# An RWKV kernel with phase mixing on one core: planned dummy matmuls, r loaded two tokens to a partition, a planner that chooses engines and load order, and w spread by a one-row matmul

## The chip, the cores and the metric

The kernel runs on one core of a Trainium2 chip. The metric is the time of one execution on the device, in microseconds (us). Single executions of one kernel scatter by about 1% here, so kernels are compared by several runs. A few executions were slow (a lower granted clock, or a time more than 1.5% above the fastest run of the same kernel).

Engines are named as in the profile: PE is TensorE (PEld its weight loads), DVE is VectorE, ACT is ScalarE, POOL is GpSimd, SP is SyncE, which issues nearly all transfers.

## The reference, cut to what matters

```python
def _attn_ref(r, k, v, w, u):            # r, k, v: (4, 8, 768, 48)   w, u: (8, 48)
    for t in range(S):
        cur = einsum('bhd,bhe->bhde', u * k_t, v_t)
        y[:, :, t] = einsum('bhd,bhde->bhe', r_t, state + cur)
        state = w * state + einsum('bhd,bhe->bhde', k_t, v_t)

def _moe_ref(x, w_theta, w_tok_r, w_tok_i, w_ch):   # x: (4, 768, 384)
    theta = x @ w_theta
    zr, zi = x * cos(theta), x * sin(theta)
    y = einsum('ts,bsd->btd', w_tok_r, zr) + einsum('ts,bsd->btd', w_tok_i, zi)
    u = x + y
    return u + maximum(u @ w_ch, 0.0)
```

The recurrence is done in chunks of 128 tokens. r is scaled by powers of w and k by inverse powers. For each batch the "front" works on three pairs of chunks: load r, k, v; scale; transpose r and k on TensorE; scores; masks; state; output; then theta, sine and cosine. "Mixing" follows: 288 matmuls of 128x384 (the groups `zr,WrT` and `zi,WiT` in the profile), more transposes, the channel matmuls, and the store.

## The kernel before: the parts that the change touches

The instructions are not written in program order. Each task is added to a `Plan` with an engine, an assumed duration in ns, its dependences and the PSUM banks it takes. A list scheduler with these assumed durations puts the tasks in order, a random search changes their priorities and keeps what shortens the planned span, and the order that results is fixed for each engine. On the chip every engine then runs its own list strictly in order.

```python
LATENCY = {PE: 200.0, DVE: 150.0, ACT: 175.0, POOL: 160.0, SP: 2200.0}
ROUNDS = 2000
# ... (inside Plan.order: the best ready task of an engine; a bank-taking task needs free banks)
                        if t.ready <= now and (
                                not t.acq or len(t.acq) + t.keep <= nfree):
                            rank = (t.prio - (STAY if e == PE and t.mode == last_mode and last_mode else 0.0), t.seq)
# ... (Plan.search: the order of the loads is not searched)
        pool = [t for t in self.tasks if t.eng != SP]
# ... (tiles: w is loaded to all partitions, and its logarithm kept beside it)
    w_f = sb.tile([C, H, D], F32, name="w_f")
    lw_f = sb.tile([C, H, D], F32, name="lw_f")
# ...
    NL = 12
    Ls = ring(NL, [C, 2 * HD], F32, "ld")       # load buffers, 3072 bytes to a partition
# ... (setup)
        P.add(SP, 300, lambda: nc.sync.dma_start(out=w_f, in_=rows_of(w, C)),
              wr=["w_f"], prio=-2e6, lat=3000)
# ... (r, k and v: two transfers of 192 KB, runs of 48 floats = 192 bytes, 1050 ns assumed for each)
        for c in range(2):
            t0 = (2 * pr + c) * C
            P.add(SP, 1050, lambda c=c, t0=t0: nc.sync.dma_start(
                out=Ls[i][:, c * HD:(c + 1) * HD].rearrange("p (h d) -> p h d", h=H),
                in_=src[b, :, t0:t0 + C, :].transpose([1, 0, 2])),
                wr=[("L", i, c)], prio=pri, lat=2200)
# ... (weights: 500 ns for each 192 KB)
        P.add(SP, 500 * n, lambda: nc.sync.dma_start(
            out=Ls[i][:, :n * HD].rearrange("p (o c) -> p o c", o=n), in_=src),
            wr=L2(i), prio=pri, lat=2200)
# ... (transposes by TensorE, eight or six blocks of 128 columns to a bank; the copy out is always ACT's)
        P.add(PE, 56 * n, go, rd=rd + ["ident"], acq=[tok], prio=prio, mode=0)
        P.add(ACT, act_ns(n * C), lambda: nc.scalar.activation(
            dst, bank16(tok)[:, :n * C].rearrange("p (a c) -> p a c", a=n), Act.Copy),
            use=[tok], wr=wr, prio=prio)
# ... (front: the copy of v to bf16 is always ACT's, the scaling of k DVE's, that of r POOL's)
            P.add(ACT, act_ns(2 * HD, False), lambda vb=vb, iv=iv: nc.scalar.activation(
                vb.rearrange("p a h d -> p (a h d)"), Ls[iv], Act.Copy),
                rd=L2(iv), wr=[kv_], prio=pb + 1)
# ... (mixing: KEEP is 0, so a mix may take the last free bank)
                P.add(PE, 649, mix, ..., prio=pb, keep=KEEP)
# ... (the end)
    P.search(ROUNDS)
    ctx.enter_context(tc.manual_schedule())
    for t in P.order():
        t.fn()
```

## Time and profile before

The median of three runs was 149.66 us (148.32 to 149.67). The profiled run took 148.95 us, of which 147.2 lie between the first and the last instruction. TensorE is busy for 130.2 us of it, VectorE for 114.8, ScalarE for 92.0.

The page of the kernel before: first the busy time of each engine, then the span in 40 equal slices of 3.7 us, where each digit is the busy share in tenths, then the main DMA queue with its packets, MB and share of the 16 DMA engines' time.

```profile
span 147.2 us, 4185 instructions
...
PE 130.2 (89%) x1641; PEld 91.3 (62%) x1641; DVE 114.8 (78%) x220; ACT 92.0 (63%) x175; POOL 79.4 (54%) x96
...
PE   0157687999999999999989999999999999999990
...
DVE  0349869699954989999979999999899998442561
...
PEclk9999999999999999999999999999999999999999
DMA  2999988999999799899998997995000111120224
...
q1 hardware_dynamic: 81040, 24.98, 69.9%
```

TensorE is full from about the eighth slice on. Below full are the first 28 us. The DMA row is full in those same slices, and stays full for two thirds of the run.

The stretches 5 to 15, 15 to 28 and 28 to 42 us of the kernel before: length, busy us (and instructions) of each engine, granted clock, share of the DMA engines' time, GB/s.

```profile
core 0: us, PE busy (x) PEld busy (x) DVE busy (x) ACT busy (x) POOL busy (x), PEclk, DMA share, GB/s
5.00:15.00 10.00, 5.41 (x74) 4.14 (x75) 6.42 (x14) 6.32 (x11) 4.69 (x5) 1.00 1.12 221
15.00:28.00 13.00, 10.25 (x133) 8.42 (x130) 10.80 (x18) 9.54 (x17) 8.80 (x9) 1.00 0.94 261
28.00:42.00 14.00, 14.00 (x166) 11.73 (x166) 11.89 (x24) 11.69 (x27) 7.79 (x8) 1.00 0.99 309
```

(The share adds up the times of all packets that start in a stretch, so it can pass 1.)

The timeline of TensorE at the start of the kernel before: start, length, engine and line, operation, operands, and in brackets the idle time before it with what ended it.

```profile
7.20 1.04 PE L414 MATMUL bank_62<-ident,Rw_95 128*128 128x128 bf16 x8 [1.28 <-POOL Rw_95 L436]
8.65 1.07 PE L414 MATMUL bank_63<-ident,Kw_97 128*128 128x128 bf16 x8 [0.41 <-DVE Kw_97 L448]
11.41 0.29 PE L470 MATMUL bank_64<-RT_106,KT_110 64*128 64x128 bf16 x1 [1.69 <-ACT KT_110 L417]
```

Eight transposes take 1.04 us here and 0.61 us later in the run: TensorE starts at half rate. The PEclk row, at 9 throughout, does not show it.

The waits of TensorE from the first mix matmul (40.5 us) to its end, kernel before: waiter, what it waited for, us in total, times, longest.

```profile
PE bank_61 L581 <- ACT xT_142 L417: 0.7, 1, 0.7
PE bank_65 L489 <- DVE PD_113 L481: 0.2, 1, 0.2
```

Two waits in 103 us: from the first mix on, TensorE is the bound of this kernel.

### The profile page before, as it was taken

What the parts mean: (1) busy time and instruction counts of PE and PEld (TensorE: products, weight loads), DVE (VectorE), ACT (ScalarE), POOL (GpSimd) and SP (SyncE); (2) the same over time, 40 slices, a digit from 0 to 9 for tenths busy, and PEclk for the clock granted to TensorE, in tenths of its full rate; (3) what the DMA queues carried; (4) which work ended last, traced back from release to release, by engine and by line L of the source; (5) the groups of instructions that cost most, each with busy time, mean ns of one, the idle gap of its engine ahead of it and who ended that gap; (6) DMA issues with size and microseconds to landing.
All of it is one profiled execution on the core that took longest, in us unless ns stands there. A gap on an engine that the chain in (4) does not pass through costs nothing.

```text
span 147.2 us, 4185 instructions
## 1 busy us (share of the span) xinstructions
PE 130.2 (89%) x1641; PEld 91.3 (62%) x1641; DVE 114.8 (78%) x220; ACT 92.0 (63%) x175; POOL 79.4 (54%) x96
## 2 busy tenths in 40 slices
PE   0157687999999999999989999999999999999990
PEld 0036574879966776667746666677666666656640
DVE  0349869699954989999979999999899998442561
ACT  3484667878949368689473984899735467702140
POOL 7317937473735649868469779691552747400000
PEclk9999999999999999999999999999999999999999
DMA  2999988999999799899998997995000111120224
GB/s 71 225 216 223 255 188 299 296 393 403 224 178 196 172 192 222 182 220 237 181 235 160 203 219 176 229 224 184 4 0 0 58 53 58 53 107 0 73 92 160
DMA packets 81084, 25.24 MB, mean 172 GB/s; under 512 B 75561, under 2 KB 79529, under 8 KB 81065
## 3 DMA queue, kind: packets, MB, share of 16 engines
q1 hardware_dynamic: 81040, 24.98, 69.9%
q8 instruction: 13, 0.21, 0.6%
q14 instruction: 7, 0.05, 0.1%
q10 hardware_dynamic: 24, 0.00, 0.0%
HBM read 20.25 MB, written 4.72 MB: 170 GB/s over the span
## 4 chain that ended last, share of the span: by engine, by line
PE 74%; DVE 7%; ACT 7%; DMA 6%; issue 3%; SPq 1%; DVEq 0%; ACTq 0%
PE bank_64 L613 8%; PE bank_65 L613 7%; PE bank_68 L613 4%; DMA ld_87<-in_v_dram 3%; DMA ld_86<-in_r_dram 3%; PE bank_63 L613 3%; PE bank_62 L613 3%; PE bank_68 L414 2%; PE bank_63 L414 2%; PE bank_63 L581 2%; PE bank_67 L613 2%; PE bank_61 L629 2%; PE bank_66 L414 2%; PE bank_64 L581 1%; PE bank_66 L613 1%
## 5 line engine op out<-in xcount | busy, mean ns | idle before, releaser
L613 PEld LDWEIGHTS <-WrT 128*128 128x128 bf16 x144 | 14.0, 97 | 7.8
L613 PEld LDWEIGHTS <-WiT 128*128 128x128 bf16 x144 | 14.1, 98 | 7.2
L526 POOL TENSOR_TENSOR Z_122<-Y_120,wC 128x192 f32<-128x192 f32 x12 | 7.8, 649 | 7.2 <-DVE Y_120 L521 4.0
L613 PE MATMUL bank_64<-zr_135,WrT 128*128 128x384 bf16 x30 | 9.8, 326 | 0.0
L613 PE MATMUL bank_64<-zi_137,WiT 128*128 128x384 bf16 x30 | 9.8, 326 | 0.0
L526 POOL TENSOR_TENSOR Z_123<-Y_121,wC 128x192 f32<-128x192 f32 x8 | 4.9, 617 | 7.3 <-DVE Y_121 L523 7.3
L613 PE MATMUL bank_65<-zr_135,WrT 128*128 128x384 bf16 x24 | 7.8, 327 | 0.0
L613 PE MATMUL bank_65<-zi_137,WiT 128*128 128x384 bf16 x24 | 7.8, 326 | 0.0
L436 POOL TENSOR_TENSOR Rw_95<-ld_88,wpow 128x384 bf16<-128x384 f32 x4 | 4.8, 1208 | 4.2 <-PE bank_67 L414 4.2
L436 POOL TENSOR_TENSOR Rw_96<-ld_85,wpow 128x384 bf16<-128x384 f32 x6 | 5.9, 1004 | 0.7 <-DMA ld_85<-in_r_dram 0.7
L594 POOL TENSOR_TENSOR zi_137<-x_132,sin_139 128x384 bf16<-128x384 bf16 x4 | 3.7, 932 | 4.3 <-ACT sin_139 L585 4.3
L613 PE MATMUL bank_62<-zi_138,WiT 128*128 128x384 bf16 x18 | 5.9, 326 | 0.0
L613 PE MATMUL bank_62<-zr_136,WrT 128*128 128x384 bf16 x18 | 5.9, 326 | 0.0
L594 POOL TENSOR_TENSOR zi_137<-x_134,sin_139 128x384 bf16<-128x384 bf16 x4 | 3.8, 964 | 3.6 <-ACT sin_139 L585 3.6
L315 PE MATMUL bank_61<-ident_f,wu 8*128 8x8 f32 x1 | 0.2, 239 | 5.7 <-DMA wu<-in_u_dram 5.7
L581 PEld LDWEIGHTS <-xT_142 128*128 128x128 bf16 x36 | 3.3, 98 | 2.6 <-ACT xT_142 L417 0.8
L594 POOL TENSOR_TENSOR zi_138<-x_132,sin_140 128x384 bf16<-128x384 bf16 x4 | 3.6, 913 | 2.4 <-ACT sin_140 L585 2.3
L414 PEld LDWEIGHTS <-Rw_95 128*128 128x128 bf16 x48 | 3.6, 111 | 2.0 <-POOL Rw_95 L436 1.4
L581 PEld LDWEIGHTS <-xT_141 128*128 128x128 bf16 x36 | 3.5, 103 | 2.1 <-issue 0.3
L436 POOL TENSOR_TENSOR Rw_96<-ld_91,wpow 128x384 bf16<-128x384 f32 x4 | 4.0, 998 | 1.5 <-DMA ld_91<-in_r_dram 0.8
L470 PEld LDWEIGHTS <-KT_110 64*128 64x128 bf16 x96 | 3.1, 101 | 2.7 <-ACT KT_110 L417 2.0
L436 POOL TENSOR_TENSOR Rw_95<-ld_94,wpow 128x384 bf16<-128x384 f32 x4 | 4.3, 1071 | 0.8 <-DVE Kw_98 L448 0.8
(593 smaller groups left out, 505.1 us busy)
## 6 DMA issues: line engine op xcount, KB each, us to landing
out_dram<-fin_150 SPq DMA_DIRECT2D x8, 192.0 KB, 2.0
out_dram<-fin_149 SPq DMA_DIRECT2D x8, 192.0 KB, 3.1
out_dram<-fin_151 SPq DMA_DIRECT2D x8, 192.0 KB, 2.0
ld_85<-in_r_dram SPq DMA_DIRECT2D x6, 192.0 KB, 4.6
ld_86<-in_k_dram SPq DMA_DIRECT2D x6, 192.0 KB, 3.6
ld_87<-in_v_dram SPq DMA_DIRECT2D x6, 192.0 KB, 4.0
ld_88<-in_r_dram SPq DMA_DIRECT2D x4, 192.0 KB, 4.1
ld_89<-in_k_dram SPq DMA_DIRECT2D x4, 192.0 KB, 3.6
```

Of the source, the lines that this page charges most:

```text
L315: nc.tensor.matmul(bank("wu")[:, :2 * HP], wu.rearrange("p a d -> p (a d)"), ident_f[:2 * HP, :2 * HP], is_transpose=True, start=True, sto ...
L414: nc.tensor.matmul(bank16(tok)[:, i * C:(i + 1) * C], s, ident, is_transpose=True, start=(i == 0), stop=(i == n - 1))
L436: lambda c=c, vec=vec, Rw=Rw, ir=ir: vec.tensor_mul(Rw[:, c, :, :D], Ls[ir][:, c * HD:(c + 1) * HD].rearrange("p (h d) -> p h d", h=H), wpow),
L470: nc.tensor.matmul(bank(tk[hi])[:, hp * C:(hp + 1) * C], KT[q, c, hp, :], RT[q, c, hp, :], start=(hp == 0), stop=(hp == HP - 1))
L526: P.add(POOL, pool_ns(HP * D) - 70, lambda cc=cc: nc.gpsimd.tensor_mul(Zs[cc % 2], Ys[cc % 2], wide(wC, D)), rd=[("Y", cc % 2), "wC"], wr= ...
L581: nc.tensor.matmul(bank(th)[:, :HD], xT[:, t, dk, :], Wth[:, dk, :], start=(dk == 0), stop=(dk == ND - 1))
L594: P.add(POOL, pool_ns(HD), lambda sn=sn, to=to, t=t: nc.gpsimd.tensor_mul(zi[:, to], x[:, to], sn[:, t]), rd=xk + [("sin", g % 2, t)], wr= ...
L613: nc.tensor.matmul(bank(tm)[:, :HD], WT[:, so, to * C:(to + 1) * C], z[:, so], start=(so == 0 and i == 0), stop=(so == NCH - 1 and i == 1))
L629: nc.tensor.matmul(bank(tf)[:, :HD], uT[:, dk, :], Wch[:, dk, :], start=(dk == 0), stop=(dk == ND - 1))
```

## The change

Its intent: fill the gaps that the plan foresees on TensorE with dummy matmuls so that its clock rises early; halve the number of small packets of r; shorten the path to the powers of w; and let the search choose the engine of many copies and products, and the order and buffer of the loads. The parts of the diff that matter, with cuts marked (`...`):

```diff
-ROUNDS = 2000
-LATENCY = {PE: 200.0, DVE: 150.0, ACT: 175.0, POOL: 160.0, SP: 2200.0}
+LATENCY = {PE: 200.0, DVE: 130.0, ACT: 190.0, POOL: 130.0, SP: 2000.0}
+SLACK = 150.0
+FILL, MARGIN, COLD = 56.0, 200.0, 5000.0
+BEGIN = 800.0
+ROUNDS = 1500
...
+    def fill(self, out, make):
+        ... (the times at which each bank is in use)
+        got, free = [], BEGIN + 400.0
+        for t in out:
+            if t.eng == PE:
+                gap = t.start - free - MARGIN
+                unit = FILL if free > COLD else 2 * FILL
+                for i, s in enumerate(spans):
+                    if gap >= unit and all(b <= free - 150 or a >= t.start for a, b in s):
+                        got.append(make(i, int(gap / unit)))
+                        break
+                free = t.start + t.ways[PE][0]
+            got.append(lambda t=t: t.fn(t.eng))
...
         pool = [t for t in self.tasks if t.eng != SP]
+        loads = [t for t in self.tasks if t.eng == SP and t.acq]
+        multi = [t for t in pool if len(t.ways) > 1]
...
+            some += rnd.sample(loads, rnd.choice((0, 0, 0, 1, 2)))
+            turn = rnd.sample(multi, rnd.choice((0, 0, 1, 2))) if multi else []
...
+            for t in turn:
+                t.eng = rnd.choice([e for e in t.ways if e != t.eng])
...
+    ones = sb.tile([1, C], F32, name="ones")
+    idle = sb.tile([C, C], BF16, name="idle")
-    w_f = sb.tile([C, H, D], F32, name="w_f")
-    lw_f = sb.tile([C, H, D], F32, name="lw_f")
+    w_1 = sb.tile([1, HD], F32, name="w_1")
-    tok_f = sb.tile([C, 2], F32, name="tok_f")
-    wpow = sb.tile([C, H, D], F32, name="wpow")
+    tok_i = sb.tile([C, 2], I32, name="tok_i")
+    tok_f = sb.tile([C, 4], F32, name="tok_f")
+    wpow = sb.tile([C, 2, H, D], F32, name="wpow")
...
+        P.add([(PE, 660)], lambda e: nc.tensor.matmul(bank("lw")[:, :HD], ones, w_1, start=True,
+                                                      stop=True),
...
+        return fetch(890, [(half(c), src[b, :, t0 + c * C:t0 + (c + 1) * C, :].transpose([1, 0, 2]))
+                           for c in range(2)])
+    def load_two(b, pr, src):
+        t0 = 2 * pr * C
+        return fetch(1400, [(lambda L: L.rearrange("p (h n) -> p h n", h=H),
+                             src[b, :, t0:t0 + 2 * C, :].rearrange("h (p n) d -> p h (n d)", n=2))])
...
+        return fetch(510 * n, [(lambda L: L[:, :n * HD].rearrange("p (o c) -> p o c", o=n), src)], late)
...
-            P.add(ACT, act_ns(2 * HD, False), lambda vb=vb, iv=iv: nc.scalar.activation(
+            P.add([act(2 * HD, False), dve(2 * HD, 2.0, True), pool(2 * HD)],
...             (likewise for the copies out of PSUM and the products in SBUF)
-                  rd=[rT] + [("Sb", b % 2, 2 * pr + c - 1) for c in cq],
+                  rd=[rT] + mk + [("Sb", b % 2, 2 * pr + c - 1) for c in cq],
...
-                      wr=[] if part == 0 else [tm], prio=pb, keep=KEEP)
+                      wr=[tm] if part else [], prio=pb, keep=4,
+                      watch=[(n, zj, s) for n in ("zr", "zi") for s in range(NCH)])
...
+    def filler(i, n):
+        def go():
+            for _ in range(n):
+                nc.tensor.matmul(bank_t[i][:, :C], idle, idle, start=True, stop=True)
+        return go
+    for go in P.fill(P.order(), filler):
+        go()
```

The planner's assumed cost of a transfer falls: a half of k or v from 1050 to 890 ns, a pair of chunks of r from 2 x 1050 to 1400 ns, the latency from 2200 to 2000.

## The prediction

> **What bounds it now.** The table of stretches shows TensorE busy 5.4 of the first 15 us, 3.15 of 15-20, 4.1 of 20-25, then fully; from 28 to 141.4 us its timeline has two gaps, 0.69 and 0.23 us. So there are three terms: a start (TensorE unfilled or slow until 28 us), a solid stretch of 113 us, a tail of 5.8 us (last matmuls, sum, store). VectorE (114.8 us busy) and the DMA queues (70%, nearly full from 5 to 105 us) sit just below.
>
> The start is doubly slow. Until about 27.6 us matmuls run at half rate: eight 128-column transposes take 1.03-1.06 us, later 0.61; three theta matmuls 1.13, later 0.65. The granted clock column stays at 1.00 and does not show this. The Trainium skill ("TensorE: Matmul & The Clock Gate", Part 1) says that the clock doubles only after some 3.4 us of sustained activity; this trace agrees, since gaps of 1.3 and 1.7 us recur until 20 us.
>
> **What the change does.**
> - 186 dummy matmuls, 176 of them ahead of the second k transposes, so TensorE should be warm by the first r transposes. That removes 0.4-0.5 us per group of 8 transposes and 0.5 per theta; some 3-4 us of it lie on the start's chain, the rest hides behind VectorE.
> - w by a one-row load and a K=1 matmul instead of a 192 KB load: powers of w near 5 us instead of 6.07. The search however puts a v load ahead of the first r, so r lands near 6 us as before: 0-0.5 us.
> - The second activation table load (1.28 us at 8.13, ahead of the first r eviction) still stands there in the order; it gains only if it runs while ACT waits for r.
> - r in runs of 384 B instead of 192 B: 12,288 packets fewer of 81,084. The trace moves about 220 GB/s in token slices, 390-400 where long weight rows load; "DMA: Bandwidth & Descriptors" (Specifications) puts line rate at 512 B and up. Alone worth little, but TensorE running 6 us earlier would otherwise overtake the loads.
> - Real TensorE work is the same 1,641 matmuls (one swapped in); mode switches rise from 68 to 77 (about 0.1 us each, 0.9 us lost). VectorE gets 20 more instructions, ACT 13 fewer.
>
> **Sum.** I estimate the second k transposes at 15.5 us (17.7 before), TensorE full from there. Remaining: 112 us of the solid stretch, 4.5 us that before had done earlier, 0.9 of switches, 1.5-2 of stalls (the weight rows land only near 33 us). TensorE ends near 135; tail 5.8; span 141; time is span plus 1.8: 142.7 us, 4.6% faster. First mix matmul near 34 us instead of 40.5; the rest is the same, shifted.
>
> Range 139.5 to 146.5. Faster by over 2%: 0.90; within 2%: 0.09; slower: 0.01.
>
> **Right if:** r transposes x8 take about 0.6 us from the first on; first mix at 33-35.5 us; from there to the end about 106 us (106.7 before); tail unchanged; DMA packets near 69,000. **Wrong if** transposes stay at 1 us, if first mix comes early and the gain is lost later (new gaps), or if the stretch after first mix itself shrinks.
>
> **What would break it:** fillers that wait on a bank still being evicted and hold up real work; v loaded first delaying the start; gaps from loads between 40 and 100 us; more collisions of VectorE and GpSimd.

## The result, and the profile after

The kernel after takes 156.26 us (median of 4 runs, 155.19 to 156.49) against 149.13 us. Ratios here are the mean time of one kernel's fast runs over that of the kernel before's fast runs of the same rounds, so not quite the ratio of the quoted medians. The ratio is 1.047, with a 95% interval of 1.039 to 1.055: slower by 4.7%, where 4.6% faster was predicted.

The page of the kernel after, the same rows:

```profile
span 154.3 us, 4560 instructions
...
PE 142.0 (92%) x1829; PEld 100.2 (65%) x1829; DVE 120.8 (78%) x240; ACT 84.7 (55%) x162; POOL 75.8 (49%) x95
...
PE   7999999789988899949999999999999999999990
...
DVE  2336889797939999787799999997999996735460
...
DMA  4999989999999999999999992012100102121114
...
q1 hardware_dynamic: 68418, 24.78, 68.4%
```

TensorE now looks full from the first slice on, but 186 of its instructions are dummies. There are 12,622 packets fewer in the main queue, as intended, and yet its share of the DMA engines' time is hardly lower: 68.4% of a longer span. Share times 16 engines times span over packets gives the time of a mean packet: 0.699 x 16 x 147.2 / 81,040 = 20.3 ns before, 0.684 x 16 x 154.3 / 68,418 = 24.7 ns after. That could be the longer packets of r, or something else; experiment e5 tells.

The same stretches of the kernel after:

```profile
5.00:15.00 10.00, 9.76 (x138) 9.05 (x137) 5.11 (x13) 5.73 (x9) 2.37 (x2) 1.00 1.25 238
15.00:28.00 13.00, 12.12 (x209) 10.51 (x207) 11.40 (x21) 7.48 (x14) 8.70 (x10) 1.00 0.99 265
28.00:42.00 14.00, 12.46 (x180) 10.24 (x180) 12.44 (x26) 9.09 (x22) 7.98 (x8) 1.00 1.01 303
```

VectorE and GpSimd do less in the first stretch than before (5.11 and 2.37 us against 6.42 and 4.69): the work that matters starts later. In the third stretch TensorE, which was full before, has 1.5 us of gaps.

The timeline of the kernel after, lines of TensorE and one of GpSimd:

```profile
5.83 4.45 PE L756 MATMUL bank_63<-idle 128*128 128x128 bf16 x40
...
7.34 1.36 POOL L532 TENSOR_TENSOR Rw_97<-ld_86,wpow 128x384 bf16<-128x384 f32 x1 [3.24 <-DMA ld_86<-in_r_dram]
...
10.07 0.75 PE L514 MATMUL bank_63<-ident,Rw_97 128*128 128x128 bf16 x8
...
17.16 0.61 PE L514 MATMUL bank_63<-ident,Rw_98 128*128 128x128 bf16 x8
17.60 3.35 PE L756 MATMUL bank_61<-idle 128*128 128x128 bf16 x57
20.79 0.61 PE L514 MATMUL bank_64<-ident,Kw_100 128*128 128x128 bf16 x8
```

The clock did rise: the first transposes take 0.75 us, the second 0.61. But the first begin at 10.07 us instead of 7.20. r landed at 7.2 us because the search had put a v load ahead of it (6.08 before), and its product was ready at 8.7. From then until 10.07 TensorE was working off 40 dummies, which ran at 107 to 111 ns each because the clock was still low (4.45 us for the 40), while the plan (constant `COLD`, after 5 us) had counted them at 56 ns.

The waits of TensorE from the first mix matmul (41.9 us) on, kernel after:

```profile
PE bank_67 L514 <- DVE x_135 L660: 1.2, 1, 1.2
PE bank_62 L709 <- ACT dg_128 L352: 0.9, 1, 0.9
PE bank_65 L639 <- ACT dg_130 L352: 0.7, 1, 0.7
PE bank_61 L604 <- ACT vb_106 L352: 0.6, 1, 0.6
```

These gaps are new; the prediction had named them as a danger. The timeline shows what stood behind the second of them, at 50.70 us:

```profile
49.73 0.84 ACT L352 ACTIVATE vb_107<-ld_93 128x768 bf16<-128x768 f32 x1 [2.21 <-DMA ld_93<-in_v_dram]
50.48 0.17 ACT L352 ACTIVATE dg_128<-bank_62 128x16 f32<-128x16 f32 x1
...
50.80 1.01 ACT L352 ACTIVATE RT_108<-bank_63 128x1024 bf16<-128x1024 bf16 x1
```

ScalarE waited 2.21 us for a v load. The 0.17 us copy that TensorE needed had to wait behind it, since each engine keeps to its list. The profile's list of waits names only `dg_128`; the load is one step further back.

The table shows where TensorE's time went until it ended. Each row is a sum over its instructions in the trace: the idle time before them, the time taken by dummies, and by all else ("real"). The columns after the first two are experiments told below.

| us | before | after | e12: before + dummies | e9: after, aligned, fixed load order | e16: after, aligned, old planner settings |
|---|---|---|---|---|---|
| first mix begins | 40.5 | 41.9 | 39.8 | 39.6 | 40.3 |
| until then: idle | 12.3 | 3.7 | 5.7 | 4.0 | 2.8 |
| until then: dummies | 0 | 13.6 | 11.6 | 12.1 | 14.0 |
| until then: real | 28.2 | 24.6 | 22.5 | 23.5 | 23.6 |
| after it: idle | 1.0 | 4.5 | 0.6 | 3.3 | 0.9 |
| after it: dummies | 0 | 0.7 | 0.2 | 0.2 | 0.2 |
| after it: real | 102.1 | 103.1 | 102.8 | 103.7 | 103.0 |
| TensorE ends | 143.6 | 150.2 | 143.4 | 146.8 | 144.4 |

After minus before is 6.6 us: real work fell by 2.6 us in all (less of it at half rate), idle time and dummies until the first mix rose by 5.0, and idle time and dummies after it by 4.2. So the warm clock was had, and more than given back.

### The profile page after: what moved, and what is told of

Same layout as the page of the kernel before. It is cut to its first block, busy times and chain, and to the rows that moved or that the text cites. A ratio compares the mean times of both kernels' runs of the same rounds, so it can differ in the third digit from the quotient of the medians.

```text
span 154.3 us, 4560 instructions
## 1 busy us (share of the span) xinstructions
PE 142.0 (92%) x1829; PEld 100.2 (65%) x1829; DVE 120.8 (78%) x240; ACT 84.7 (55%) x162; POOL 75.8 (49%) x95
## 3 DMA queue, kind: packets, MB, share of 16 engines
q1 hardware_dynamic: 68418, 24.78, 68.4%
## 4 chain that ended last, share of the span: by engine, by line
PE 67%; DMA 12%; ACT 6%; DVE 5%; issue 5%; POOL 2%; SPq 0%; ACTq 0%
PE bank_61 L709 5%; PE bank_62 L709 4%; PE bank_66 L709 4%; PE bank_65 L709 4%; PE bank_68 L709 4%; DMA ld_87<-in_v_dram 4%; PE bank_61 L756 3%; DMA ld_93<-in_v_dram 3%; PE bank_63 L756 3%; DMA ld_96<-in_v_dram 3%; DMA ld_89<-in_moe_w_ch_dram 2%; PE bank_64 L709 2%; PE bank_63 L514 2%; PE bank_63 L727 2%; PE bank_64 L514 1%
## 5 line engine op out<-in xcount | busy, mean ns | idle before, releaser
L756 PEld LDWEIGHTS <-idle 128*128 128x128 bf16 x186 | 13.8, 115 | 2.3 <-issue 1.1
L709 PE MATMUL bank_62<-zr_137,WrT 128*128 128x384 bf16 x24 | 7.8, 327 | 1.2 <-ACT dg_128 L352 0.9
L756 PE MATMUL bank_61<-idle 128*128 128x128 bf16 x106 | 7.7, 233 | 1.1 <-DVE idle L360 1.1
L352 ACT ACTIVATE uT_150<-bank_62 128x384 bf16<-128x384 bf16 x2 | 1.0, 499 | 12.6 <-PE bank_62 L514 12.6
L709 PE MATMUL bank_62<-zi_139,WiT 128*128 128x384 bf16 x24 | 7.8, 326 | 0.0
L532 POOL TENSOR_TENSOR Rw_98<-ld_90,wpow 128x384 bf16<-128x384 f32 x3 | 3.0, 1004 | 6.6 <-DMA ld_90<-in_r_dram 5.2
L545 DVE TENSOR_TENSOR Kw_99<-ld_87,wpinv 128x384 bf16<-128x384 f32 x4 | 3.4, 859 | 1.9 <-DMA ld_87<-in_k_dram 1.9
L677 PEld LDWEIGHTS <-xT_143 128*128 128x128 bf16 x36 | 3.3, 97 | 2.5 <-ACT xT_143 L352 0.5
L677 PEld LDWEIGHTS <-xT_144 128*128 128x128 bf16 x36 | 3.3, 98 | 2.3 <-ACT xT_144 L352 0.5
L532 POOL TENSOR_TENSOR Rw_98<-ld_95,wpow 128x384 bf16<-128x384 f32 x4 | 3.9, 998 | 1.2 <-PE bank_61 L654 1.2
L756 PE MATMUL bank_63<-idle 128*128 128x128 bf16 x40 | 4.4, 314 | 0.0
L578 DVE TENSOR_TENSOR PD_114<-RT_108,KT_112 128x1024 bf16<-128x1024 bf16 x3 | 2.0, 683 | 3.0 <-ACT KT_112 L352 3.0
L532 POOL TENSOR_TENSOR Rw_97<-ld_93,wpow 128x384 bf16<-128x384 f32 x3 | 3.3, 1101 | 2.1 <-DMA ld_93<-in_r_dram 2.1
```

The source lines that it names most:

```text
L352: nc.scalar.activation(dst, src, Act.Copy)
L532: P.add(two_inputs(HD) if g else two_inputs(HD)[::1 - 2 * n], lambda e, n=n, Rw=Rw, ir=ir: vec[e].tensor_mul(Rw[:, n, :, :D], load(ir).rea ...
L545: P.add(two_inputs(HD)[::-1], lambda e, c=c, Kw=Kw, ik=ik: vec[e].tensor_mul(Kw[:, c, :, :D], load(ik)[:, c * HD:(c + 1) * HD].rearrange(" ...
L578: vec[e].tensor_mul(PD, RT.rearrange("p h a t -> p a h t"), KT), rd=[kT, rT], wr=[kP], prio=pb + 4)
L677: nc.tensor.matmul(bank(th)[:, :HD], xT[:, t, dk, :], Wth[:, dk, :], start=(dk == 0), stop=(dk == ND - 1))
L709: nc.tensor.matmul(bank(tm)[:, :HD], WT[:, so, to * C:(to + 1) * C], z[:, so], start=(so == 0 and i == 0), stop=(so == NCH - 1 and i == 1))
```

## The experiments

Eighteen kernels ran, in five batches; the kernels of one batch ran on one chip beside the kernel before, whose medians were 148.77, 149.33, 148.66, 149.95 and 149.40 us. (The last two of these medians include one slow run each; the ratios don't.) All results were correct except e2's. These theories were at stake, in the order in which they came up: the **dummies** hold up real work; the **loads** are later than the plan assumes; the free choice of **engines** overloads one (VectorE through it: called V); the **address** of the load buffers makes each packet slower; the new **settings of the planner** lead to worse orders.

| run | median us | ratio to before, 95% interval |
|---|---|---|
| after | 156.26 | 1.047 (1.039 to 1.055) |
| e1 no dummies | 156.88 | 1.052 (1.046 to 1.058) |
| e2 r, k, v as long rows (wrong result) | 150.68 | 1.012 (1.007 to 1.018) |
| e3 old load costs in the plan | 151.97 | 1.022 (1.016 to 1.028) |
| e4 engines fixed | 158.75 | 1.070 (1.062 to 1.078) |
| e5 aligned | 152.46, 151.96 (fast runs) | 1.020 (1.013 to 1.026) |
| e6 before, shifted by 32 bytes | 150.57 | 1.011 (1.003 to 1.019) |
| e7 aligned, no dummies | 152.72, 152.19, 152.08 (fast runs) | 1.020 (1.015 to 1.026) |
| e8 aligned, old load costs | 151.94 | 1.018 (1.012 to 1.024) |
| e9 aligned, fixed load order | 151.98 | 1.022 (1.016 to 1.028) |
| e10 aligned, another seed | 153.10 | 1.029 (1.022 to 1.037) |
| e11 before, another seed | 149.96 | 1.008 (1.000 to 1.016) |
| e12 before with dummies | 148.73, 148.16, 150.14 (fast runs) | 1.003 (0.991 to 1.015) |
| e13 before with r two tokens to a partition | 151.25 | 1.011 (1.003 to 1.018) |
| e14 aligned, r as before | 158.83 | 1.062 (1.054 to 1.069) |
| e15 aligned, old bank rules | 152.30, 153.19 (fast runs) | 1.021 (1.008 to 1.033) |
| e16 aligned, old planner settings | 149.51 | 0.997 (0.989 to 1.006) |
| e17 as e16, engines free | 150.56 | 1.008 (1.004 to 1.012) |
| e18 aligned, engines fixed | 155.01 | 1.039 (1.034 to 1.043) |

### e1: no dummies

```diff
-    for go in P.fill(P.order(), filler):
-        go()
+    for t in P.order():
+        t.fn(t.eng)
```

> The changed kernel with its plan untouched, the dummy matmuls left out. Theory L (the plan counts on loads that land earlier than they do, and TensorE, which runs in order, stands waiting for them): the dummies sit mostly in time that is lost anyway, so 154 to 158 us; the first transposes go back to 1.0 us per eight. Theory F (the dummies hold real matmuls up; in the trace 40 of them ran at 110 ns each until 10.28 us, while the first r transposes had their input at 8.7): 150 us or less. Theory E (engines chosen badly): about 156.

Measured: 1.052. Taking the dummies away does not recover the loss; if anything it costs half a point. The held transposes at 10.07 us are real but are not what made the kernel slow, and the warm clock is worth at most that half point: without dummies TensorE idles 10.4 us between its first instruction and the first mix, instead of 2.7 idle and 13.6 spent on dummies, and the median is 0.6 us later. The dummy theory falls for the loss.

### e2: r, k and v read as long contiguous rows

```diff
-            return lambda L: L[:, c * HD:(c + 1) * HD].rearrange("p (h d) -> p h d", h=H)
+            return lambda L: L[:, c * HD:(c + 1) * HD]
...
-        return fetch(890, [(half(c), src[b, :, t0 + c * C:t0 + (c + 1) * C, :].transpose([1, 0, 2]))
+        return fetch(890, [(half(c), flat(src, b, HD)[2 * pr + c])
```

The same plan, instruction for instruction, and the same bytes, but in runs of 1536 or 3072 bytes. The data land in the wrong places and the result is wrong.

> Same plan, same dummies, same number of loads and bytes, but r, k and v are read as if they lay in contiguous rows (wrong result on purpose), so each load should take about half the time. Theory L: the waits for loads go, 147 us or less, first mix matmul before 38 us instead of 41.9. Theories F and E: 152 us or more, because neither dummies nor engine choices change.

Measured: 1.012. Some 5.4 of the 7.1 us vanish with nothing changed but the duration of the transfers: the queue holds 14,658 packets and takes 48.3% of the DMA engines' time, and idle time after the first mix falls from 4.5 to 1.7 us. So most of the loss comes through the loads. The expectation of the loads theory was still missed: it had 147 us or less and a first mix before 38 us, and the first mix came at 40.3. With loads this much shorter the new order does not beat the old one, which says that a gain was not merely hidden behind the loads.

### e3: the old load costs in the plan

```diff
-LATENCY = {PE: 200.0, DVE: 130.0, ACT: 190.0, POOL: 130.0, SP: 2000.0}
+LATENCY = {PE: 200.0, DVE: 130.0, ACT: 190.0, POOL: 130.0, SP: 2200.0}
-        return fetch(890, [
+        return fetch(1050, [
-        return fetch(1400, [
+        return fetch(2100, [
```

(The 2300 ns latency of the first load goes too.)

> Only the plan's costs of loads go back to those of before (1050 ns per half of k or v, 2100 for r, latency 2200, instead of 890, 1400, 2000) and the plan is searched anew. Theory L: 146 to 151 us. Theory F: 154 or more, the dummies stay. Theory E: 154 or more.

Measured: 1.022. A plan made with slower loads loses 4.3 us less on the same hardware, though its 151.97 us lie above the 146 to 151 that the loads theory had expected. The landing times in the traces show how wrong the new costs were: halves of k in the kernel after land 1.05 us apart (8.25 and 9.30 us) where the plan has 0.89, and 384 KB of r take 2.05 us (5.14 to 7.19) where it has 1.4. Before, halves landed 0.86 us apart (seven of them from 5.23 to 10.41 us) where its plan had 1.05. The old plan was generous, the new one too tight. But why does a 192 KB half, the same transfer in both kernels, take 0.86 us in one and 1.05 in the other? That question led to e5.

### e4: engines fixed

```diff
-        multi = [t for t in pool if len(t.ways) > 1]
+        multi = []
```

> The search may no longer move a task to another engine; each keeps its first one, close to before. Theory L: within 1.5% of the changed kernel (154 to 158). Theory E: 151 or less. Theory F: 154 or more.

Measured: 1.070, slower than the kernel after by 2.3 points. The free choice of engines helps the new planner; it isn't the cause of the loss here.

### e5: the load buffers moved by 32 bytes

In the kernel before the load buffers begin at byte 24,384 of a partition, a multiple of 64. The change made the tiles ahead of them larger, the allocator pads only to 32 bytes, and they now begin at 25,184, which is 32 more than a multiple of 64. Each buffer is 3072 bytes long, so all twelve are off alike. One unused tile of 32 bytes puts them back; the plan stays the same.

```diff
+    sb.tile([C, 8], F32, name="pad")
     Ls = ring(NL, [C, 2 * HD], F32, "ld")
```

> The changed kernel and its plan untouched; an unused tile of 32 bytes a partition ahead of the load buffers moves them (and all tiles after them) from addresses that are 32 modulo 64 to multiples of 64, as the kernel before has them. In the trace of before 192-byte packets took 15.5 ns on average with a median of 15; in the changed kernel 18.0 with a tail of 25 to 36. Theory A (the new small tiles moved the load buffers off 64-byte multiples, and that slows each 192- or 384-byte write): 192-byte packets 15.5 ns, 384-byte ones 22 to 23, time 148 to 152 us. Theory L alone (the plan's load costs are too low whatever the address): packets stay at 18 ns and the time at 154 to 157.

Measured: 1.020 from the two fast runs, 152.46 and 151.96 us. Two of its four executions were slow (196.47 us, clock 0.668, which is also the profiled one, and 154.82), so its trace is read for the packets alone. 32 unused bytes are worth about 4 us of the 7.1. e7, e8 and e9, also aligned, were made from it and agree.

### e6: the kernel before, shifted by 32 bytes

The reverse: the same line put into the kernel before, which moves its buffers to 32 more than a multiple of 64.

> The kernel before, its plan untouched, with the same 32-byte tile: now its load buffers are at 32 modulo 64. Theory A: 192-byte packets 18 ns, waits for loads appear, 150 to 155 us. Theory L alone: 148 to 149.5, packets 15.5 ns.

Measured: 1.011. The order and the packets are the same as before, and the main queue of the shifted kernel shows what changed:

```profile
span 148.9 us, 4185 instructions
...
PE 130.2 (87%) x1641; PEld 90.5 (61%) x1641; DVE 115.7 (78%) x220; ACT 92.1 (62%) x175; POOL 78.3 (53%) x96
...
q1 hardware_dynamic: 81040, 24.98, 78.0%
```

78.0% instead of 69.9% of the DMA engines' time for the same 81,040 packets: 22.9 ns against 20.3 for a mean packet. Taken by size from the records of the packets, a 192-byte packet takes 15.5 ns in the kernel before and 18.4 ns shifted; 18.0 ns in the kernel after and 15.3 to 15.6 ns in the aligned ones. It isn't an even shift: 2% of these packets take over 1.1 times the median of 15 ns when aligned, 26 to 28% (25 to 36 ns each) when not. A 384-byte packet takes 24.8 ns in the kernel after and 23.2 to 24.1 aligned. So the address makes packets slower in both kernels. Halves now land 1.05 us apart (from 6.57 to 10.78 us), just what the old plan had assumed, which is why the kernel before loses only some 1.4 us by it while the kernel after, planned for 0.89, loses 4. What the shift also does, moving every tile behind the buffers by 32 bytes, is the same in e5 and e6; the packets of the loads are what the records show to change, while VectorE, ScalarE and GpSimd take about the time that they took before (114.8, 92.0 and 79.4 us).

### e7: aligned, no dummies

> As the aligned one, without the dummy matmuls; same plan. With loads early again, theory F (dummies hold the first transposes up, by 1.4 us in the trace) would make this one as fast as or faster than the aligned one; if warm clocks are worth more than that, it is 1 to 3 us slower.

Measured: 1.020 from three fast runs (the profiled one was slow, 319.46 us), the same as e5. With the loads back at their rate, 186 dummies and a warm clock are worth nothing that could be measured here.

### e8: aligned, old load costs

The edits of e5 and e3 together.

> Aligned, and the plan searched with the load costs of before. Theory A alone: within 1% of the aligned one, since aligned loads come about as planned. If the plan's costs are still too low for aligned loads (a k or v load of 384 KB took 1.9 us in before, the plan says 1.78; r 1.4), it is 1 to 3 us faster than the aligned one: 146 to 149.

Measured: 1.018, the same as e5. Two cures for one illness: a plan that allows for slow loads, or loads that are not slow. Together they give no more than each alone. About 2% remain, and neither is their cause.

### e9: aligned, the loads in fixed order

```diff
-        loads = [t for t in self.tasks if t.eng == SP and t.acq]
+        loads = []
-            some += rnd.sample(loads, rnd.choice((0, 0, 0, 1, 2)))
```

> Aligned (as above), and the search may no longer move loads: they are issued in the order in which the program names them (r, k, v of the first pair first), still into whichever buffer is free. Theory O (the searched load order, which puts a v load ahead of the first r, costs the start): first r transposes by 9 us instead of about 9.7, time 149 to 151. If the order does not matter: 151.5 to 153.

Measured: 1.022. r is loaded first again, lands at 4.55 us, and the first transposes start at 7.1 us as before the change. The first mix starts 0.9 us earlier than before, at 39.6. And yet the kernel ends 3 us later than before, all of it after the first mix: 3.3 us idle against 1.0, and 1.6 us more of real work that is left for then. The order of the loads isn't the cause of the rest, and an early start does not carry through to the end.

Its main queue, to be set against that of the kernel after:

```profile
span 150.2 us, 4500 instructions
...
q1 hardware_dynamic: 68418, 24.78, 63.6%
```

0.636 x 16 x 150.2 / 68,418 = 22.3 ns for a mean packet, 24.7 in the kernel after with the same packets.

### e10 and e11: another seed of the search, aligned and before

```diff
-    P.search(ROUNDS)
+    P.search(ROUNDS, 1)
```

> Aligned, with another seed of the search: another plan of the same kind. It tells how far two plans of one planner differ on the chip. Theory P (what is left of the slowdown is that the new planner's plans do worse on the chip): 150 to 154. Theory S (a chance of one seed): anywhere from 146 to 155, away from 152 by more than 2 us.

> The kernel before with another seed of its search. Theory P: 148 to 151, that is, plans of the old planner stay better. Theory S: 151 or more is as likely as 148.

Measured: 1.029 for the aligned kernel (1.020 with seed 0) and 1.008 for the kernel before. A new draw of the search moves either by about a point. The two do not overlap: plans of the new planner lie at 1.020 and 1.029 as it is set (e5, e10), and at 1.018 to 1.022 with one of its settings undone (e8, e9, e15); those of the old one lie at 1.000 and 1.008. So the rest is more than one unlucky draw, though two to four draws on a side are few.

### e12: the kernel before with dummies

The function `fill` and the dummies were put into the kernel before, 147 of them, 112 ns assumed for each until 11 us; the order of the real work is untouched.

> The kernel before, its plan and addresses modulo 64 untouched, with 147 dummy matmuls in the gaps of its start, costed cold until 11 us so that they do not hold up real work. The prediction took 3 to 4 us from warm clocks in the start: then 145 to 147. If the start is bound by VectorE, ScalarE and loads and not by TensorE: 148 to 149.5, although the transposes there take 0.55 us instead of 1.0.

Measured: 1.003 (0.991 to 1.015), no difference that three fast runs can show (the fourth, 151.06 us, was slow). This is the cleanest test of the gain that the prediction rested on. The stretches of this kernel:

```profile
core 0 of [0], span 147.0 us
...
5.00:15.00 10.00, 7.64 (x111) 6.92 (x111) 6.32 (x13) 6.20 (x12) 4.46 (x5) 1.00 1.09 214
15.00:28.00 13.00, 12.18 (x238) 10.45 (x237) 11.46 (x20) 10.62 (x19) 8.32 (x10) 1.00 0.94 237
28.00:40.00 12.00, 11.40 (x140) 9.87 (x140) 11.23 (x23) 9.66 (x22) 5.81 (x6) 1.00 1.04 363
```

TensorE reaches its full rate by about 13 us instead of 28. Its real work until the first mix shrinks from 28.2 to 22.5 us. The first mix starts at 39.8 us instead of 40.5, and the span is 147.0 us instead of 147.2. The other 5 us turned into dummies and idle time, because the work was not there yet: VectorE does 6.32 us in the first stretch where it did 6.42, 11.46 in the second where it did 10.80, and the DMA share is 0.94 or more, as before. At the start TensorE is not the bound, so making it faster there buys next to nothing.

### e13: the kernel before with r two tokens to a partition

The layout of r alone (the load in runs of 384 bytes at the old planner's 2100 ns, the doubled powers of w, the order of the transposed r), planned anew by the old planner, with aligned buffers.

> The kernel before with one part of the change alone: r by two tokens to a partition (packets of 384 bytes), its powers of w and its transposes' eviction to match; load buffers kept on 64-byte multiples; old planner. If the layout of r is harmless or helps: 147 to 149.5. Theory R (the layout of r costs: one load of 384 KB lands later than the first of two halves, the eviction writes every other element): 150.5 to 152.5, as the aligned kernels of the change.

Measured: 1.011, slightly slower. The queue takes 65.1% instead of 69.9% of the DMA engines' time, so the saving is real: one 384-byte packet at about 24 ns against two of 192 at 15.5. But the kernel was not short of this, and r now comes as one load: the product of the first chunk cannot start on the first half, and the first transposes begin at 8.1 us instead of 7.2. That this is what costs the point isn't shown: the plan is a new one, its first mix begins early, at 35.1 us, and another seed alone moved the kernel before by 0.8 points (e11).

### e14: aligned, r as before

The reverse, in the new planner: r in two halves of 192-byte runs, at the new cost of 890 ns each.

> The changed kernel, aligned, with r loaded as before (one token to a partition, two loads of 192-byte packets); new planner and the rest of the change. Theory R: 149 to 150.5. If the layout of r helps loads: 153 to 155. If it does not matter: 151.5 to 153.

Measured: 1.062, 6.5 us slower than the aligned kernel, with 6.5 us of idle time after the first mix. So r's layout, worth nothing in the old plan, went with a large gain in the new. Why is not shown. Load costs that are too low would be a ready answer, but aligned halves landed 0.86 us apart in the kernel before and this plan has 0.89; and the plan is again a new draw of the search. (The trace also shows TensorE at half rate for 3.4 us in the middle of this run, as in e3, e8 and e18; e8 is no slower for it than its like.)

### e15: aligned, the old bank rules

```diff
-                      wr=[tm] if part else [], prio=pb, keep=4,
+                      wr=[tm] if part else [], prio=pb, keep=0,
-                  rd=[rT] + mk + [("Sb", b % 2, 2 * pr + c - 1) for c in cq],
+                  rd=[rT] + [("Sb", b % 2, 2 * pr + c - 1) for c in cq],
```

> The changed kernel, aligned, without two new rules of the planner: mix may again take banks when few are free (keep is 0), and the carried products no longer wait for all masks. Theory K (these rules hold TensorE up after the first mix): idle time after first mix falls from 3.3-4.8 us to about 1, time 148.5 to 150.5. Otherwise 151.5 to 153.5.

Measured: 1.021 from two fast runs of four (152.30 and 153.19; the profiled one was slow). The rule that mixing leaves four banks free, and the wait of the carried products for the masks, do not explain the rest by themselves.

### e16: aligned, old planner settings

The edits of e3, e4, e5, e9 and e15 together. What stays of the change: the dummies, r two tokens to a partition, w by a one-row matmul, and the rest of the new planner: how it treats the port that VectorE and GpSimd share, its other assumed durations, buffers chosen by the plan, and 1500 rounds.

> Aligned, and the planner as near to the old one as its switches allow: no new rules, old load costs, loads in program order, engines fixed. What stays of the change: dummies, r's layout, w by the K=1 matmul, rest of the new planner (port handling, latencies, fewer rounds). Theory V (moving tasks onto VectorE, whose work rises from 128 to 136 us, is what costs): 148.5 to 150. If engine freedom helps, as it did unaligned: 152 to 155.

Measured: 0.997 (0.989 to 1.006): the whole loss is gone, and there is no gain. (It is one draw of the search.) After the first mix TensorE idles 0.9 us, as before the change. Its waits after 41 us:

```profile
PE bank L514 <- DVE mAT L572: 0.4, 2, 0.3
PE bank L567 <- DVE mAT L572: 0.2, 1, 0.2
```

So the rest of the loss lies in the settings of the planner that were undone here. The parts of the change that alter the work on the chip, taken together with what stays of the planner, are worth nothing that could be measured: neither good nor bad.

### e17: as e16, engines free

> As e16 (aligned; old rules, old load costs, loads in program order), but the search may move tasks to other engines. Theory V (the freedom of engines is what costs the last 3 us, through VectorE): 151.5 to 153, with VectorE busy over 120 us. If rules, load costs and load order together are the cause: 148.5 to 150.5.

Measured: 1.008 (1.004 to 1.012). With the other settings old, the free choice of engines costs about a point at most; VectorE is then busy for 127.3 us, more than in any other kernel. Idle time after the first mix is 0.9 us.

### e18: aligned, engines fixed

> The changed kernel, aligned, with engines fixed and nothing else changed (new rules, new load costs, free load order stay). Theory V: 148.5 to 150.5. If rules, load costs and load order together are the cause: 152 to 156 (unaligned, fixing the engines made it 2.5 us slower).

Measured: 1.039 (1.034 to 1.043), 1.9 points slower than e5, as e4 was slower than the kernel after. The theory that the rest comes from free engines by way of a fuller VectorE falls: with the new settings the freedom helps, with the old ones it costs at most the point that another seed can cost too.

## Why the prediction was wrong, point by point

- **"eight 128-column transposes take 1.03-1.06 us, later 0.61"; "TensorE should be warm by the first r transposes"**: nearly right. The first took 0.75 us, the next 0.61, and full rate came at about 10 us instead of 28. The Trainium skill ("TensorE: Matmul & The Clock Gate", Part 1) gives 107 ns for a 128-column matmul at the low clock and 56 ns at the high one. The trace agrees: 40 dummies took 4.45 us cold (111 ns each), 57 took 3.35 us warm (59).
- **"That removes 0.4-0.5 us per group of 8 transposes and 0.5 per theta; some 3-4 us of it lie on the start's chain"**: this is the first step that failed. The time was removed (real work until the first mix fell by 3.6 us after, by 5.7 us in e12), but it lay on no chain that decided the end: e12 gained 0.7 us at the first mix and 0.2 us of span. In the first 28 us TensorE was the engine that waited. The page showed it, in a DMA row that is full from the second slice, and in a VectorE busy 10.8 of 13 us. The prediction's first paragraph even says that the queues are "nearly full from 5 to 105 us", and then costs the start by TensorE alone. The same page of the skill calls the cost of the ramp under 1% of a typical span; e12 agrees as far as it goes: rate doubled at about 13 us instead of 28, and no gain (1.003, 0.991 to 1.015).
- **"I estimate the second k transposes at 15.5 us (17.7 before), TensorE full from there"**: measured at 20.8 us. Of this, 57 dummies in the way account for some 0.7 to 1.0 us (the last product was ready at 19.8); for the rest, the second pair of k had landed only at 16.5 us, since v and a 384 KB block of token weights went ahead of it.
- **"First mix matmul near 34 us instead of 40.5"**: 41.9 us. Nor is the first mix a measure of the end: in e13 it began at 35.1 us, with no dummies at all, in e10 at 37.8, and both runs were longer than before. The "4.5 us that before had done earlier" were counted as the only price of an early start; the work that the plan leaves for later, and the idle time that comes with it, had to be counted as well.
- **"1.5-2 of stalls"; "from there to the end about 106 us (106.7 before)"**: 112.4 us. Idle time after the first mix is 4.5 us alone. Part of it comes from loads that land later than the plan's order needs: with loads made fast (e2) 1.7 us are left. Aligned buffers alone do not remove it in the other plans of the new planner (2.9 us in e8, 3.3 in e9, 4.7 in e10); with the planner's old settings it is 0.9 us (e16, e17). (e5's own trace is of a slow run and cannot tell.)
- **Not in the prediction at all: the address of the load buffers.** It explains about 4 of the 7.1 us. The diff showed it to whoever adds up the tiles.
- **Not costed: the plan's assumed durations.** The diff lowers them openly, and the trace of before had the measured 0.86 us for a half; 0.89 is not wrong against that. With the new address it became wrong, 1.05 us.
- **"What would break it"**: the list held three of the things that happened (dummies that hold real work, v loaded first, gaps from loads between 40 and 100 us). A slower result was nevertheless given 1%. The first two turned out to matter little; the third mattered most.
- **"DMA packets near 69,000"**: right, 68,463. **"powers of w near 5 us instead of 6.07"**: hardly; the two that r now needs were computed from 4.96 to 6.01 us, against 5.47 to 6.07 for the one before, and the inverse power that k needs was done at 6.48 instead of 5.56. r was not there until 7.2. The table load did run while ScalarE waited for r. None of these shortened the run. **"Tail 5.8"**: the prediction's tail, last matmuls included, is 5.8 us before; from TensorE's end to the end of the span it is 3.6 us before and 4.1 after.

What is shown: the loss of 7.1 us is some 4 us of buffer address, made costly by a plan with tight load costs, and some 3 us of the planner's new settings; the dummies, the layout of r and the matmul for w bring nothing together (e16), and the dummies nothing by themselves (e7, e12). What stays open: how the 3 us divide. Load costs (e8), load order (e9) and bank rules (e15), each undone alone, change nothing; all three together (e17) bring about a point; the engines fixed as well (e16) another; the engines alone (e18) make it worse. As a new seed moves a plan by about a point (e10, e11), single differences of a point between plans can't be laid to the setting that was changed. That the search runs 1500 rounds instead of 2000 over a wider space was not tested, nor were the planner's other durations and its treatment of the shared port by themselves.

No version beats the kernel before. e16 equals it.

## What to carry to other kernels

Before pricing a faster engine, ask in each stretch which row is full: a gap on an engine whose inputs come from full queues is a sign of waiting, and filling it or speeding up its work there returns as more waiting. In a kernel whose order is fixed by a plan, the assumed durations are part of the design: here costs that were slightly too high left slack (the shift of 32 bytes cost the kernel before 1.1%), and costs that were too low let late loads hold up what stood behind them (the same shift cost the kernel after 2.7 points). And when a change adds or drops small tiles, look at where the buffers of the loads now begin.

## What the Trainium skill lacked or had wrong

- "DMA: Bandwidth & Descriptors" (Specifications, and "How a descriptor splits into AXI transactions") speaks of packets under 512 bytes being slow and of the 256-byte alignment at which a descriptor's reads start, but not of the start of the SBUF buffer that is loaded. Here 192-byte packets took 15.3 to 15.6 ns into buffers at multiples of 64 bytes and 18.0 to 18.4 ns at 32 more; the same packets took 69.9% or 78.0% of the DMA engines' time. The fast buffers begin at 64 or 128 bytes past a multiple of 256, both slow ones at 96, so 64 as the number that counts is an inference.
- The same page's 512 bytes for line rate: no run here has packets of 512, but the sizes around it fit. A mean 192-byte packet took 15.5 ns (12 bytes/ns), 384 bytes about 24 ns (16), and in e2 1536 bytes 72 ns and 3072 bytes 138 ns (21 and 22).
- "TensorE: Matmul & The Clock Gate" (Part 1) gives some 3.4 us of sustained activity for the clock to rise. In the kernel after, TensorE was at work almost without a break from 1.06 us and was at full rate only at about 10.4 us; in the kernel before it stayed at half rate until about 28 us, though its last gap of over 1 us ended at 17.1; with dummies in the kernel before the rise came at about 13 us. What does not count as activity, or whether the 1.64 us of the one-row fp32 matmul does (the plan had 0.66 us for it), no run here separates.
- No page names the profile's PEclk row, which stays at 9 or 1.00 while TensorE runs at half rate in the first 28 us of the kernel before (eight transposes in 1.04 us, later 0.61).
